# Row maxima transposed before they are split, and eight stores back on one queue, in an attention and Fourier-mixing kernel

## The chip, the cores and the metric

The kernel runs on one core of a Trainium2 chip. The metric is the time of one execution on the device in microseconds (us); of several executions the median counts. Engines are named as the profile names them: PE is TensorE's matmuls, PEld its weight loads, DVE is VectorE, ACT is ScalarE, POOL is GpSimd, SP is SyncE. SPq and ACTq are the queues from which SP and ScalarE issue DMAs. `L735` is line 735 of the kernel before.

## What is computed

Two stages, for a batch of 8, 8 heads, 576 rows, 64 values per head and 128 features. The output has 8 x 576 x 512 fp32 values.

```python
def phi(x):
    proj = np.einsum('bhsd,df->bhsf', x, w_phi)
    proj = proj - np.max(np.abs(proj), axis=-1, keepdims=True)
    return np.concatenate([np.exp(proj), np.exp(-proj)], axis=-1)
q_p, k_p = phi(q), phi(k)
kv  = np.einsum('bhsf,bhsd->bhfd', k_p, v)
num = np.einsum('bhsf,bhfd->bhsd', q_p, kv)
den = np.einsum('bhsf,bhf->bhs', q_p, np.sum(k_p, axis=2))[..., None] + 1e-06
x = (num / den)                      # heads side by side: 8 x 576 x 512
u = x + np.real(np.fft.fft(np.fft.fft(x, axis=1), axis=2))
un = (u - mean(u)) / np.sqrt(var(u) + 1e-06)
out = u + np.maximum(un @ w_ch1, 0.0) @ w_ch2       # 512 -> 2048 -> 512
```

The maximum over the absolute projections of a row is what this change handles: for the queries of the first batch it is needed as a row vector, along the free dimension of a matmul.

## The kernel before

**Stages.** For each of the 8 batches the kernel loads q, k and v, projects them on the features, exponentiates, forms the key-value products per head (tile `kv`, copied to `kvh`), combines them with the queries' features (`pn_`, divided into the tile `X`), folds the rows (`R`, `CEO`), applies the Fourier matrices (`psD`, `pu`), normalises (`UN`, `UT`) and runs the two layers (`psf`, `pso`), whose result is added into `X` and stored.

**Order.** The stages of neighbouring batches are interleaved by a written plan: a string of letters, each of which runs one step of a stream (M mixing, F the two layers, T the features, P the queries' maxima, and so on). A step issues its instructions to the engines in program order; each engine works off its own instructions in that order and waits on semaphores. Y is a step of matmuls whose result nobody reads (tile `idle`).

**Tiles.** PSUM has three pools: `pj` (two buffers), `pk` (one) and `pb` (three). A DMA issued from SP or ScalarE takes one of eight completion semaphores in turn, and waits for the DMA that had it before.

**The first batch** has its own functions, in `first_features`. The queries' negative features are exp(-(proj)) with the maximum taken off twice inside PSUM: `negative` and `last_rows` add, to the projection in `psn` or `ph4`, matmuls that pick a row of maxima (weights `pick`, a column with -2 in three places 32 rows apart, L697 and L717). The maxima come from `widest` and `widest4` (projection `psq`, reduced by L755 and L772 into the fp32 tile `MQ`), for the outer heads (pairs 0 and 3) first and the inner heads (pairs 1 and 2) later. Each time `turn_m` turns the 20 columns of maxima into rows. It splits them into three bf16 parts in SBUF (L730 to L733: high part, remainder, middle part, low part, into the tile `m3`), transposes the three together with one bf16 matmul against the identity (L735, into `pt`), and casts the result into the bf16 tile `mt` (L740). [...] After `turn_m` for the inner heads come, on DVE, the reciprocals and products of the first combines (L951, L953).

**The last batch.** `store` writes rows of `X` when the second layer has been added: chunk 1 in eight DMAs of 64 KB (L1201), chunks 0 and 3 in one of 256 KB with chunk 2 (L1207). In the last batch the eight alternate between SP's and ScalarE's queue:

```python
for a in range(8):
    queue = nc.scalar if b == B - 1 and a % 2 else nc.sync
    queue.dma_start(...)
```

Then follow chunk 3 (L1207 on SP) and the last 64 rows in two halves of 256 columns: `forward` stores the first half from ScalarE and the second from SP (both L1280), with one row of each from ScalarE (L1281).

Of the kernel before, what the change touches and what calls it, by code (L numbers as in the profile page):

```python
# [10 lines left out]
ALU = mybir.AluOpType  # L11
AX = mybir.AxisListType
F32 = mybir.dt.float32
BF16 = mybir.dt.bfloat16
# [26 lines left out]
def kernel(  # L41
# [10 lines left out]
    nc = tc.nc  # L52
    B, H, S, D = q.shape
# [11 lines left out]
    const = ctx.enter_context(tc.tile_pool(name="const", bufs=1))  # L65
# [4 lines left out]
    small = ctx.enter_context(tc.tile_pool(name="small", bufs=2))  # L70
# [4 lines left out]
    pk = ctx.enter_context(tc.tile_pool(name="pk", bufs=1, space=PSUM))  # L75
# [10 lines left out]
    wphi2 = const.tile([128, DF], BF16, name="wphi2")  # L86
# [24 lines left out]
    MQ = [const.tile([128, H, 5], F32, name=f"MQ{i}") for i in range(2)]  # L111
# [13 lines left out]
    ident = const.tile([128, 128], F32, name="ident")  # L125
# [5 lines left out]
    nc.vector.memset(keep[64:65], 0.0)  # L131
    pick_i = const.tile([96, 32], I32, name="pick_i")
    pick = const.tile([96, 32], BF16, name="pick")
    m3 = const.tile([128, 3, 32], BF16, name="m3")
    nc.vector.memset(m3[:], 0.0)
    ident_b = const.tile([128, 128], BF16, name="ident_b")

    def count(out, pattern, base, mult):
# [184 lines left out]
    def load_first():  # L323
# [36 lines left out]
        QT4 = attn.tile([128, 4, 64], BF16, tag="QT4", name="QT4")  # L360
        turned_k[0], turned_q[0] = (KT, KT4), (QT01, QT23, QT4)
        parts[0] = first_features()

    def turn_part(dst, blocks, by_act):
# [271 lines left out]
    def first_features():  # L636
        QT01, QT23, QT4 = turned_q[0]
        KT, KT4 = turned_k[0]
        V, V4_ = values[0]
        mq = MQ[0]  # L640
        KPp = attn.tile([128, H, 4, DF], BF16, tag="KPp", name="KPp")
        KPn = attn.tile([128, H, 4, DF], BF16, tag="KPn", name="KPn")
        K4p = attn.tile([128, 4, DF], BF16, tag="K4p", name="K4p")
# [6 lines left out]
        tiles, rows_of_m = {}, {}  # L650

        def half(x, outer):
            return x[:, 0:4:3] if outer else x[:, 1:3]

        def by_pair(x):
            return x.rearrange("p (x e) n -> p x e n", e=2)

        def project(ps, t, outer, last):
            for x, pr in enumerate((0, 3) if outer else (1, 2)):
                for jj in range(2):  # L660
                    rr = slice(64 * jj, 64 * jj + 64)
                    rq = (QT01, QT23)[t][rr, 2 * pr:2 * pr + 2, :]
                    rq = rq.rearrange("p h (a r) -> p h a r", r=16)
                    rq = rq[:, :, :, ::-1] if t else rq[:, :, ::-1, :]
                    nc.tensor.matmul(
                        ps[:, jj, 2 * x:2 * x + 2, :], lhsT=wphi2[rr, :], rhs=rq,
                        start=last or x == 0, stop=last,
                    )
# [9 lines left out]
        def result(t, outer, QP, ps, sgn):  # L678
            if outer:
                return rows_of(t, outer, QP, ps, sgn)  # L680
            o = QP[:, 2:6, 256 * t:256 * t + 256].rearrange("p h (c s) -> p c h s", c=2)
            nc.scalar.activation(out=o[:, ::-1] if t else o, in_=ps[:], func=AT.Exp, scale=sgn)
# [6 lines left out]
        def negative(t, outer):  # L689
            ps = pj.tile([128, 2, 4, 128], F32, tag="pj", name="psn")  # L690
            project(ps, t, outer, False)
            m = rows_of_m[outer][:].rearrange("p (a r) -> p a r", r=16)
            m = m[:, :, ::-1] if t else m[:, ::-1, :]
            for jj in range(2):
                for x in range(4):
                    k_ = 5 * x + 2 * t + (1 - jj if t else jj)
                    nc.tensor.matmul(  # L697
                        ps[:, jj, x, :], lhsT=pick[:, k_:k_ + 1].to_broadcast([96, 128]), rhs=m,
                        start=False, stop=(x == 3),
                    )  # L700
            result(t, outer, QPHN, ps, -1.0)
# [22 lines left out]
            nc.scalar.activation(out=o, in_=i, func=AT.Exp, scale=sgn)  # L724

        def turn_m(outer):
            m = half(mq[:].rearrange("p (x e) c -> p x (e c)", e=2), outer)
            left = small.tile([128, 2, 10], F32, tag="ml", name="ml")
            hi, mid, lo = (m3[:, i, 0:20].rearrange("p (x n) -> p x n", x=2) for i in range(3))
            nc.vector.tensor_copy(out=hi, in_=m)  # L730
            nc.vector.tensor_tensor(out=left[:], in0=m, in1=hi, op=ALU.subtract)
            nc.vector.tensor_copy(out=mid, in_=left[:])
            nc.vector.tensor_tensor(out=lo, in0=left[:], in1=mid, op=ALU.subtract)  # L733
            pt = pk.tile([96, 128], F32, tag="pk", name="pt")
            nc.tensor.matmul(  # L735
                pt[:], lhsT=m3[:].rearrange("p a b -> p (a b)"), rhs=ident_b[:],
                start=True, stop=True,
            )
            mt_ = small.tile([96, 128], BF16, tag="mt", name="mt")
            nc.vector.tensor_copy(out=mt_[:], in_=pt[:])  # L740
            rows_of_m[outer] = mt_

        def widest(t, outer):
            ps = [pb.tile([128, 4, DF], F32, tag="pb", name="psq") for jj in range(2)]
            for x, pr in enumerate((0, 3) if outer else (1, 2)):
                for e in range(2):
                    for jj in range(2):
                        rr = slice(64 * jj, 64 * jj + 64)
                        nc.tensor.matmul(
                            ps[jj][:, 2 * x + e, :], lhsT=(QT01, QT23)[t][rr, 2 * pr + e, :],  # L750
                            rhs=wphi2[rr, :], start=True, stop=True,
                        )
            for jj in range(2):
                c = 2 * t + (1 - jj if t else jj)
                nc.vector.tensor_reduce(  # L755
                    out=half(by_pair(mq[:])[:, :, :, c], outer),
                    in_=ps[jj][:].rearrange("p (x e) f -> p x e f", e=2), axis=AX.X, op=ALU.max,
                    apply_absolute_value=True,
                )

        def widest4():
            ps = [pb.tile([64, 4, DF], F32, tag="pb", name="psq4") for e in range(2)]
            for pr in range(4):
                for e in range(2):
                    rr = slice(64 * e, 64 * e + 64)
                    nc.tensor.matmul(
                        ps[e][:, pr, :], lhsT=QT4[rr, pr, :], rhs=wphi2[rr, :],
                        start=True, stop=True,
                    )
            m = mq[0:64, :, 4].rearrange("p (pr e) -> p e pr", e=2)  # L770
            for e in range(2):
                nc.vector.tensor_reduce(  # L772
                    out=m[:, e], in_=ps[e][:], axis=AX.X, op=ALU.max, apply_absolute_value=True
                )

        def maxima():
            yield widest(0, True)
            yield widest(1, True)
            yield widest4()
            yield turn_m(True)  # L780
            yield widest(0, False)
            yield widest(1, False)
            yield turn_m(False)
# [32 lines left out]
        def steps():  # L816
            yield keys4()
            for pr in PAIRS:
                yield from keys(pr)
            yield positive(0, True)  # L820
            yield positive(1, True)
            yield last_rows(QPHP, 1.0, None)
            yield negative(0, True)
            yield negative(1, True)
            yield last_rows(QPHN, -1.0, True)
            yield positive(0, False)
            yield positive(1, False)
            yield negative(0, False)
            yield negative(1, False)
            yield last_rows(QPHN, -1.0, False)  # L830
# [366 lines left out]
    def store(b, U, c):  # L1197
        if c == 1:
            for a in range(8):
                queue = nc.scalar if b == B - 1 and a % 2 else nc.sync  # L1200
                queue.dma_start(  # L1201
                    out=out[b, 225 - 32 * a:257 - 32 * a, :].rearrange("(r j) n -> r j n", j=2),
                    in_=U[16 * a:16 * a + 16, 0:2, 0:C],
                )
        elif c in (2, 3):
            rows_ = out[b, 320:576, :].rearrange("(a r j) n -> a r j n", r=16, j=2)
            nc.sync.dma_start(out=rows_[:, ::-1, 3 - c, :], in_=U[:, c, 0:C])  # L1207
        elif c == 4:
            nc.sync.dma_start(out=out[b, 257:320, :], in_=U[1:64, 4, 0:C])
            nc.sync.dma_start(out=out[b, 0:1, :], in_=U[0:1, 4, 0:C])  # L1210

    def forward(b):
# [80 lines left out]
        for g in (0, 64):  # L1293
            nc.vector.scalar_tensor_tensor(
                out=U[0:64, 4, 0:C], in0=po[g:g + 64, :], scalar=scale_of[b, 4][0:64],
                in1=U[0:64, 4, 0:C], op0=ALU.mult, op1=ALU.add,
            )
        store(b, U, 4)
        yield

# [108 lines left out]
```

## Time and profile before

| | |
|---|---|
| median of 3 runs | 426.7 us (426.19 to 426.71) |
| the profiled execution's own time | 426.19 us |
| its span, first to last instruction | 424.3 us |
| PE busy | 399.3 us (94%) |
| PEld busy | 255.9 us (60%) |
| DVE busy | 330.8 us (78%) |
| ACT busy | 306.0 us (72%) |
| POOL busy | 207.8 us (49%) |
| granted TensorE clock, mean | 0.995 |

The span is what the profile covers; the execution's own time is 1.9 us longer. Busy shares are averages over the whole span. The page follows the chain of work that ended last back from the last instruction and gives the shares of its engines. A timeline line has the start and the length in us, the engine, the source line, the operation, the tiles (written <- read), the shapes, and in brackets the idle time of that engine before it with what ended it. For a line that merges several instructions (x8) the length goes from the first start to the last end. The lines of DMA queues give the time that issuing took, not the transfer.

### The profile page before, as it was taken

The numbers are of one execution on the slowest core, as the hardware profiler recorded it, in microseconds if no ns is written. First come the engines' busy times: TensorE is split into PE (matmuls) and PEld (weight loads), VectorE is DVE, ScalarE is ACT, GpSimd is POOL, SyncE is SP. The second block draws the span as 40 slices with busy tenths as digits, with TensorE's granted clock in tenths as the row PEclk, the third lists the DMA queues.
The fourth block names the chain that finished last, engine by engine and source line by source line (L and its number), as shares of the span: only waits on it lengthen the run. The fifth ranks groups of instructions, "written<-read, shape, count | busy, mean of one in ns | idle before, by whom it ended". The sixth has DMA issues, their size and how long they took to land.

```text
span 424.3 us, 10395 instructions
## 1 busy us (share of the span) xinstructions
PE 399.3 (94%) x4093; PEld 255.9 (60%) x4122; DVE 330.8 (78%) x682; ACT 306.0 (72%) x626; POOL 207.8 (49%) x271
## 2 busy tenths in 40 slices
PE   8797798999899999999999999999999999999995
PEld 3365475744676558655676558565766567656562
DVE  4889788798979976998779895998999796968103
ACT  6888799748975899489847887588868887353460
POOL 7983588526656077706682282744755341500000
PEclk9899999999999999999999999999999999999999
DMA  8999949974669459953999059953894051103313
GB/s 218 202 167 174 149 76 170 145 86 78 89 113 179 65 97 109 126 76 56 116 153 126 7 101 127 122 71 62 119 139 76 14 102 32 27 0 72 72 26 87
DMA packets 108699, 42.70 MB, mean 101 GB/s; under 512 B 82859, under 2 KB 103595, under 8 KB 108651
## 3 DMA queue, kind: packets, MB, share of 16 engines
q0 software_dynamic: 45936, 16.60, 35.8%
q1 hardware_dynamic: 62287, 25.05, 33.7%
q8 instruction: 32, 0.52, 0.5%
q10 hardware_dynamic: 428, 0.39, 0.3%
q14 instruction: 16, 0.13, 0.1%
HBM read 36.77 MB, written 9.44 MB: 109 GB/s over the span
## 4 chain that ended last, share of the span: by engine, by line
PE 63%; DVE 22%; ACT 9%; DMA 2%; issue 2%; POOL 0%; DVEq 0%; ACTq 0%
PE psf L1223 21%; PE pso L1240 19%; DVE R L903 3%; DVE cb L999 3%; PE kv L887 3%; PE idle L1340 3%; DVE tg L994 3%; PE psD L1045 2%; DMA UT<-UN 2%; PE pso L1287 2%; PE pu L1104 2%; PE psq L547 1%; DVE MK L511 1%; PE psk L491 1%; PE psh L597 1%
## 5 line engine op out<-in xcount | busy, mean ns | idle before, releaser
L1223 PE MATMUL psf<-UT,W1b 128*128 128x320 bf16 (+1 forms) x1024 | 142.5, 286 | 2.6 <-DMA UT<-UN 1.8
L1240 PE MATMUL pso<-W2b,HT 128*128 128x512 bf16 x483 | 120.6, 379 | 1.7 <-issue 0.5
L1223 PEld LDWEIGHTS <-W1b 128*128 128x128 bf16 x1024 | 94.0, 98 | 29.9 <-issue 4.1
L1240 PEld LDWEIGHTS <-HT 128*128 128x128 bf16 x512 | 46.4, 98 | 46.4 <-issue 2.6
L1228 ACT ACTIVATE HT<-psf 128x320 bf16<-128x320 f32 x128 | 53.5, 442 | 27.0 <-PE psf L1223 21.6
L1002 POOL TENSOR_TENSOR X<-cb,rd 128x320 f32<-128x320 f32 x56 | 41.6, 746 | 39.3 <-DVE rd L1001 38.0
L466 POOL TENSOR_TENSOR VCn<-VS,VCn 128x512 bf16<-128x512 bf16 x28 | 29.7, 1062 | 38.1 <-ACT VCn L461 35.3
L1230 ACT ACTIVATE HT<-psf 128x512 bf16<-128x512 f32 x64 | 37.9, 605 | 12.9 <-PE psf L1223 12.3
L555 DVE TENSOR_REDUCE MQ<-psq 128x8 f32<-128x1024 f32 (+1 forms) x32 | 34.3, 1085 | 13.6 <-PE psq L547 13.4
L1246 DVE SCALAR_TENSOR_TENSOR X<-pso,rs,X 128x512 f32<-128x512 f32 x32 | 23.6, 736 | 24.4 <-PE pso L1240 24.4
L497 ACT ACTIVATE KPn<-psk 128x1024 bf16<-128x1024 f32 x28 | 28.6, 1021 | 14.6 <-DVE MK L511 14.6
L497 ACT ACTIVATE KPp<-psk 128x1024 bf16<-128x1024 f32 x28 | 28.7, 1025 | 11.1 <-PE psk L491 11.1
L451 POOL TENSOR_TENSOR V4N<-VS,V4N 64x256 bf16<-64x256 bf16 x14 | 8.7, 624 | 54.5 <-ACT V4N L447 54.0
L511 DVE TENSOR_REDUCE MK<-psk 128x8 f32<-128x1024 f32 x28 | 33.9, 1213 | 1.0 <-ACT KPp L497 0.7
L1094 DVE TENSOR_TENSOR X<-pu,X 128x512 f32<-128x512 f32 (+3 forms) x49 | 23.3, 526 | 11.2 <-PE pu L1104 8.9
L466 POOL TENSOR_TENSOR VCp<-VS,VCp 128x512 bf16<-128x512 bf16 x28 | 29.7, 1059 | 0.0
L606 ACT ACTIVATE QPHP<-psh 128x1024 bf16<-128x1024 f32 x28 | 28.9, 1031 | 0.8 <-PE psh L597 0.6
L606 ACT ACTIVATE QPHN<-psh 128x1024 bf16<-128x1024 f32 x28 | 29.0, 1035 | 0.0
L1150 ACT ACTIVATE UN<-X,MV 128x512 bf16<-128x512 f32 (+1 forms) x35 | 24.5, 723 | 5.4 <-DVE MV L1175 3.1
L1174 DVE BATCH_NORM_STATS2 st<-X 128x6 f32<-128x512 f32 (+1 forms) x40 | 27.1, 677 | 0.3
L1190 POOL TENSOR_TENSOR rs<-VE,mhalf 128x5 f32<-128x5 f32 (+1 forms) x9 | 10.3, 1142 | 29.2 <-DVE VE L1189 29.0
L987 PEld LDWEIGHTS <-QPHP 128*128 128x128 bf16 x280 | 21.2, 99 | 4.6 <-DVE cb L999 1.0
(465 smaller groups left out, 820.5 us busy)
## 6 DMA issues: line engine op xcount, KB each, us to landing
out_dram<-X SPq DMA_DIRECT2D x16, 256.0 KB
out_dram<-X SPq DMA_DIRECT2D x60, 64.0 KB
QS<-in_q_dram POOLq DMA_DIRECT2D x14, 256.0 KB, 6.0
KS<-in_k_dram POOLq DMA_DIRECT2D x7, 512.0 KB, 6.8
VS<-in_v_dram POOLq DMA_DIRECT2D x14, 256.0 KB, 5.1
W1b<-in_moe_w_ch_dram POOLq DMA_DIRECT2D x1, 2048.0 KB, 13.2
W2b<-in_moe_w_ch_dram POOLq DMA_DIRECT2D x1, 2048.0 KB, 16.4
W2b<-in_k_dram SPq DMA_DIRECT2D x2, 512.0 KB
```

What stands on the lines that cost most here:

```text
L466: nc.gpsimd.tensor_tensor(out=VC[:, hs, :, 0:D], in0=values[b][0][:, hs, :].rearrange("p h (j d) -> p h j d", d=D), in1=VC[:, hs, :, D:D + ...
L497: nc.scalar.activation(out=KP[:, hs, :, :].rearrange("p e (jp jj) f -> p jj (e jp) f", jj=2), in_=psk[:], func=AT.Exp, scale=sgn,)
L511: nc.vector.tensor_reduce(out=MK[:, 2 * pr:2 * pr + 2, :].rearrange("p e (jp jj) -> p jj (e jp)", jj=2), in_=tiles[pr][:], axis=AX.X, op=A ...
L555: nc.vector.tensor_reduce(out=o, in_=i[:], axis=AX.X, op=ALU.max, apply_absolute_value=True)
L606: nc.scalar.activation(out=o, in_=psh[:], func=AT.Exp, scale=sgn)
L1002: nc.gpsimd.tensor_tensor(out=X[:, :, D * h:D * h + D], in0=cb[:, :, 0:D], in1=rd[:].to_broadcast([128, 5, D]), op=ALU.mult,)
L1150: nc.scalar.activation(out=UN[0:M, c, :], in_=X[0:M, c, 0:C], func=AT.Identity, scale=-1.0, bias=mv[0:M, c, 0:1],)
L1174: nc.vector.bn_stats(out=st[0:M, :], in_=X[0:M, c, 0:C])
L1223: nc.tensor.matmul(ps, lhsT=W1b[:, cc, 128 * hh:128 * hh + 128], rhs=UT[:, cc, lo:hi], start=(cc == 0), stop=(cc == NCC - 1),)
L1228: nc.scalar.activation(out=HT[:, hh, lo:hi], in_=ps, func=AT.Relu, scale=-1.0)
L1230: nc.scalar.activation(out=HT[:, hh - 1:hh + 1, lo:hi], in_=psw[:].rearrange("p (a n) -> p a n", a=2), func=AT.Relu, scale=-1.0,)
L1240: nc.tensor.matmul(po[:], lhsT=HT[:, hh, at:at + 128], rhs=W2b[:, hh, :], start=(hh == 0), stop=(hh == NHH - 1),)
```

## The change

Two edits. In the first batch `turn_m` transposes the 20 columns of fp32 maxima first, with a TensorE transpose into PSUM (20 x 128). The split into three bf16 parts is then done on the transposed rows, from PSUM, into rows 0 to 19, 32 to 51 and 64 to 83 of a tile `mt` that is zeroed once at the start; the remainder is written back in place in PSUM. `MQ` of the first batch is viewed with the outer heads' 20 columns together and the inner heads' 20 columns together, and `widest` and `widest4` write it in that order. In the last batch the eight stores of chunk 1 all go to SP's queue.

```diff
-    m3 = const.tile([128, 3, 32], BF16, name="m3")
-    nc.vector.memset(m3[:], 0.0)
+    mt = const.tile([96, 2, 128], BF16, name="mt")
+    nc.vector.memset(mt[:], 0.0)
...
-        mq = MQ[0]
+        mq = MQ[0][:].rearrange("p (o x e) c -> p o x e c", o=2, e=2)
...
-            m = rows_of_m[outer][:].rearrange("p (a r) -> p a r", r=16)
+            m = rows_of_m[outer].rearrange("p (a r) -> p a r", r=16)
...
         def turn_m(outer):
-            m = half(mq[:].rearrange("p (x e) c -> p x (e c)", e=2), outer)
-            left = small.tile([128, 2, 10], F32, tag="ml", name="ml")
-            hi, mid, lo = (m3[:, i, 0:20].rearrange("p (x n) -> p x n", x=2) for i in range(3))
-            nc.vector.tensor_copy(out=hi, in_=m)
-            nc.vector.tensor_tensor(out=left[:], in0=m, in1=hi, op=ALU.subtract)
-            nc.vector.tensor_copy(out=mid, in_=left[:])
-            nc.vector.tensor_tensor(out=lo, in0=left[:], in1=mid, op=ALU.subtract)
-            pt = pk.tile([96, 128], F32, tag="pk", name="pt")
-            nc.tensor.matmul(
-                pt[:], lhsT=m3[:].rearrange("p a b -> p (a b)"), rhs=ident_b[:],
-                start=True, stop=True,
-            )
-            mt_ = small.tile([96, 128], BF16, tag="mt", name="mt")
-            nc.vector.tensor_copy(out=mt_[:], in_=pt[:])
-            rows_of_m[outer] = mt_
+            to = mt[:, 0 if outer else 1, :]
+            pt = pk.tile([20, 128], F32, tag="pk", name="pt")
+            nc.tensor.transpose(
+                pt[:], mq[:, 0 if outer else 1].rearrange("p x e c -> p (x e c)"), ident[:]
+            )
+            nc.vector.tensor_copy(out=to[0:20], in_=pt[:])
+            nc.vector.tensor_tensor(out=pt[:], in0=pt[:], in1=to[0:20], op=ALU.subtract)
+            nc.vector.tensor_copy(out=to[32:52], in_=pt[:])
+            nc.vector.tensor_tensor(out=to[64:84], in0=pt[:], in1=to[32:52], op=ALU.subtract)
+            rows_of_m[outer] = to
...
-                    out=half(by_pair(mq[:])[:, :, :, c], outer),
+                    out=mq[:, 0 if outer else 1, :, :, c],
...
-            for pr in range(4):
+            for x, pr in enumerate((0, 3, 1, 2)):
...
-                        ps[e][:, pr, :], lhsT=QT4[rr, pr, :], rhs=wphi2[rr, :],
+                        ps[e][:, x, :], lhsT=QT4[rr, pr, :], rhs=wphi2[rr, :],
...
-            m = mq[0:64, :, 4].rearrange("p (pr e) -> p e pr", e=2)
+            m = mq[0:64, :, :, :, 4].rearrange("p o x e -> p e (o x)")
...
             for a in range(8):
-                queue = nc.scalar if b == B - 1 and a % 2 else nc.sync
-                queue.dma_start(
+                nc.sync.dma_start(
```

## The prediction

> **What bounds the kernel now.** I read four views: the page's chain that ended last, that chain in order of time for the first 47 us, the timeline of VectorE (DVE) and TensorE (PE) around the two changed steps, and the timeline of the two store queues at the end. The page's chain summary:
>
> ```profile
> PE 63%; DVE 22%; ACT 9%; DMA 2%; issue 2%; POOL 0%; DVEq 0%; ACTq 0%
> ```
>
> TensorE carries the end, so a wait placed in front of TensorE is paid unless something else is later. The chain in order of time (start, us, what) runs through both places where the change works:
>
> ```profile
> 31.64 0.19 PE pt L735
> ...
> 32.47 0.55 PE psn L697 x8
> ...
> 34.53 0.33 PE pn__730 L944 x10
> ...
> 34.88 0.21 DVE rd L951
> ```
>
> Here TensorE works without a hole from 28.06 to 34.86, and then hands the chain to DVE. The timeline (start, us, engine, line; in brackets the idle time before it and who ended it):
>
> ```profile
> 25.41 0.29 DVE L740 CAST mt<-pt 96x128 bf16<-96x128 f32 x1 [0.35 <-PE pt L735]
> ...
> 26.10 0.62 PE L697 MATMUL psn<-mt,pick 96*128 96x128 bf16 x8
> ...
> 28.06 0.29 PE L887 MATMUL kv<-VCp,KPp 128*128 128x65 bf16 x4 [0.21 <-POOL VCp L869]
> ...
> 28.47 0.58 DVE L730 CAST m<-MQ 128x20 bf16<-128x20 f32 x1
> ...
> 29.09 0.98 DVE L731 TENSOR_TENSOR ml<-MQ,m 128x20 f32<-128x20 f32 x1
> ...
> 30.11 0.78 DVE L732 CAST m<-ml 128x20 bf16<-128x20 f32 x1
> ...
> 30.92 0.18 DVE L733 TENSOR_TENSOR m<-ml,m 128x20 bf16<-128x20 f32 x1
> ...
> 31.57 0.26 PE L735 MATMUL pt<-ident_b,m 128*96 128x128 bf16 x1
> ```
>
> The split into three bf16 parts (L730 to L733) is slow the second time, 2.63 us, yet it is over at 31.10 while TensorE comes to its matmul at 31.57; the idle time before L735's weight load is put down to issue, not to DVE. So the split is hidden; only the cast after the matmul (0.29) stands between TensorE's transpose and the matmuls L697 that read the result.
>
> The end:
>
> ```profile
> 414.82 2.56 SPq L1201 DMA_DIRECT2D out_dram<-X  x4
> 414.83 2.86 ACTq L1201 DMA_DIRECT2D out_dram<-X  x4
> 418.28 0.65 SPq L1207 DMA_DIRECT2D out_dram<-X  x1
> 419.53 0.57 ACTq L1280 DMA_DIRECT2D out_dram<-X  x1
> 420.55 0.31 SPq L1280 DMA_DIRECT2D out_dram<-X  x1
> ```
>
> No engine computes after 420.53; the stores' traffic ends at 422.7 in the trace's DMA records and the span at 424.3.
>
> **The change, part by part.** TensorE, GpSimd and ScalarE keep their order in the changed build, apart from the changed instructions; the written plan is the same.
>
> *First batch, outer heads.* The fp32 transpose stands where L735 stood, so TensorE comes to it at 25.11 as before. One fp32 128x128 transpose (L368) is 0.27 us against 0.26 for L735; I take them as equal. DVE, which before did its four small operations from 23.92 to 25.06, now idles until the transpose is done and starts at 25.41. Then come four dependent operations on 20x128 from PSUM in place of one cast. L740 is the nearest row, 0.29; L953, which reads PSUM and SBUF, takes 0.49 for 320 elements, about 1.07 ns more for each element beyond L740's 128, so 0.29 again. Dependent DVE operations follow each other with 0.03 to 0.04 between them (L731, L732, L733 start at 24.45, 24.67, 24.88 and take 0.18). Four: 0.29 + 3 x 0.32 = 1.25, done at 26.66 instead of 25.70. That is 0.96 more behind the transpose. No row shows DVE writing PSUM, or an fp32 subtraction in place there: the low bound is the 20-element row, 3 x 0.22 = 0.65; the high one is the held row L731, 3 x 1.0 = 3.0. I take 0.96, because L740 at 31.87 and L953 at 32.48 ran at 0.29 and 0.49 while GpSimd was issuing DMAs (31.19 to 33.55), the kind of company in which L732 took 0.78.
>
> [...]
>
> L697 needed the result at 26.10 and gets it at 26.70, so TensorE is held 0.6. Queued behind it are the second psq, psn and L697; the second psq also waits for a psq buffer, because the four reductions L755 start at 26.70 instead of 25.95, at most 0.1 more. Then comes L887, which now waits for GpSimd until 28.06 although the weights were ready at 27.63: 0.3 to 0.4 of the delay goes there. I carry 0.3 on.
>
> *First batch, inner heads.* TensorE reaches its transpose at 31.87 (31.57 + 0.3), DVE starts at 32.17 and is done at 33.42; L697 needs it at 32.40 and starts at 33.46: 1.06 late, the 0.3 included. DVE's own queue behind it (L951, L953, L220, to 34.72) has 0.16 idle before L951 at 34.88; it starts at 33.45 instead of 32.18, is free at about 35.8 and the fourth combine comes from TensorE at 35.93. So the chain passes 34.88 about 1.05 late. ScalarE has 1.45 of slack before HI at 41.13, so it does not add; what it waits for there is DVE, late by the same 1.05. All later work hangs on this, so nothing gives it back. The saved weight load and cast shape, the larger memset of mt at 1.04 (TensorE and GpSimd are busy without it) and the new layout of MQ cost nothing; if the memset were on the path it would be about 0.1.
>
> *Last batch.* All eight L1201 go to SP. Each is an issue of 0.6; five of the seven earlier batches show eight in 5.12 to 5.15, with the next L1207 0.1 later. So L1207 is issued at 414.82 + 5.13 + 0.1 = 420.05 instead of 418.28: 1.77 late. Its 256 KB start 1.3 after issue and flow for 2.5 (issued 402.71, traffic 404.04 to 406.54; issued 418.28, 419.56 to 422.12), so to 423.9. The last store (L1280 on SP) shares that queue. It also gets a new wait: in the changed build it takes the semaphore of ScalarE's L1280, and SP waits until that one has landed. ScalarE's was issued at 419.53 and its packets ended at 422.42, partly because L1207's were in front. If it lands at 422.3 to 422.8, SP issues 1.7 to 2.2 later than now, and its data are out 2.2 after that, or a little less with nothing in front. Bounds for this part: 1.2 (only L1207's traffic counts, less what it overlapped with) and 2.3. I take 1.85.
>
> [...]
>
> Sum: 1.05 + 1.85 = 2.9. The profiled execution took 426.19 (span 424.3 and 1.9 around it) and is the fastest of the three; from it 429.1, from the median 426.7 **429.6**, which I give.
>
> **Rivals.**
> 1. *The front is absorbed* (a later stage waits for something that the front does not move, for instance weights): 426.7 + 1.85 = 428.55. Against it: the chain from 34.88 to 110 has only engine work and relative waits. 0.10.
> 2. *The end is hidden*, only the front counts: 427.75. For it: the DMA engines have room at 415 to 416. Against it: the issue rows. 0.08.
> 3. *The clock drops.* The trace grants 0.5 from 17.45 to 20.86, after 3.4 us with only 1.75 of TensorE work; 2.05 did not do it. The hole at 40 to 42 moves by 1 us, and the stretch 41.3 to 44.8 falls from 2.74 to about 1.8. Then what lies on the path behind it (L477 0.42, L1104 0.52) doubles: 430.5. 0.08.
> 4. *Not slower.* The split leaves SBUF, where L731 was held 0.98 instead of 0.18. If DVE and not TensorE's place in the plan sets L735, then the inner step shrinks from 3.69 (28.47 to 32.16) to 0.30 + 1.25, 2.1 less, and the outer from 1.78 by 0.2; with the end's 1.85 that is 426.2, and with the end at its low bound 425.6. The front alone gains if TensorE reaches the inner transpose before 30.6, and makes up for the end if it does so by 29.0; that needs 2.6 us of work ahead of L735 to vanish, and the chain shows that work on TensorE. 0.07.
> 5. *Nothing shows*: both parts hidden, 426.7. 0.03.
>
> **How the numbers follow.** The forecast has 0.64. The range from 427.7 to 430.7 takes in rivals 1 to 3 and the bounds of the end (1.2 to 2.3, so 428.95 to 430.05); the high bound of 3.0 for each step in PSUM, which no row in such company supports, stays outside with rivals 4 and 5. About 0.85 us, 0.2%, can be told from no change. Slower by more: 0.64 + 0.10 + 0.08 + 0.08 = 0.90, less 0.01 for rival 2, which ends near the border, so 0.89; within: that 0.01, rival 5 with 0.03 and 0.03 of rival 4, so 0.07; faster: 0.04, the rest of rival 4.
>
> **What would show it.** Right: DVE idle before the first cast of pt, four rows of about 0.29, L697 at 26.7 and 33.5, L951 for the fourth combine near 35.9, SP with eight issues of 5.1 and its last store after ScalarE's has landed. Wrong: rows of 0.5 or more for the operations in PSUM (then slower still), TensorE at its transposes earlier than 25.1 and 31.5, or traffic that ends as soon after the last sum as now.

## The result

The changed kernel takes 427.75 us (median of 22 runs, 426.92 to 429.44), the kernel before on the same chip 426.24 us (22 runs, 424.91 to 427.29). The ratio is 1.0042, with a 95% interval of 1.0030 to 1.0053: 1.8 us slower, between 1.3 and 2.3 (the means are 1.8 apart, the medians 1.5). The forecast was 2.9 slower, from a base of 426.7. Two executions of one experiment below (e7) ran at granted clocks of 0.555 and 0.654 and are left out of its ratio. In the kernel after, the lines of `turn_m` are L729 and L732 to L735, and later lines have numbers smaller by 5 or 6 (kv L882, reciprocal L946, the stores L1195, L1201, L1274).

The profiled execution after took 427.3 us with a span of 425.5, that is 1.2 more span than before. The page's chain has moved a little from TensorE to DVE, and GpSimd has appeared on it:

```profile
PE 57%; DVE 25%; ACT 7%; POOL 5%; DMA 2%; issue 2%; DVEq 0%; ACTq 0%; POOLq 0%
```

The timeline of the kernel after at the first batch, DVE's and TensorE's lines (start, length, engine, line; in brackets the idle time and who ended it):

```profile
25.36 0.28 DVE L732 CAST mt<-pt 20x128 bf16<-20x128 f32 x1 [3.21 <-PE pt L729]
25.67 0.29 DVE L733 TENSOR_TENSOR pt<-pt,mt 20x128 f32<-20x128 f32 x1
...
26.31 0.28 DVE L735 TENSOR_TENSOR mt<-pt,mt 20x128 bf16<-20x128 f32 x1
26.64 0.61 PE L697 MATMUL psn<-mt,pick 96*128 96x128 bf16 x8 [0.66 <-DVE mt L735]
...
33.37 0.61 PE L697 MATMUL psn<-mt,pick 96*128 96x128 bf16 x8 [0.69 <-DVE mt L735]
...
35.84 0.20 DVE L946 RECIPROCAL rd<-pn__724 128x5 f32<-128x5 f32 x1
```

DVE idles until the transpose is done and then makes four operations of 0.28 to 0.29, as forecast; TensorE is held 0.66 and 0.69, and the chain passes the fourth combine's reciprocal at 35.84 where it passed at 34.88. This 0.96 stays: SP's store at 95.35 stood at 94.39 before, the one at 251.06 at 250.09. But the store at 273.77 stood at 273.81. The front's whole delay is gone by then.

The last batch, SP's and ScalarE's queues after:

```profile
414.77 5.12 SPq L1195 DMA_DIRECT2D out_dram<-X  x8
420.00 0.65 SPq L1201 DMA_DIRECT2D out_dram<-X  x1
421.42 0.30 SPq L1274 DMA_DIRECT2D out_dram<-X  x1
419.48 0.57 ACTq L1274 DMA_DIRECT2D out_dram<-X  x1
420.09 0.65 ACTq L1275 DMA_DIRECT2D out_dram<-X  x2
```

The eight issues take 5.12, the 256 KB store leaves at 420.00 instead of 418.28, SP's last store at 421.42 instead of 420.55. In the trace's landing records the last landing comes at 424.35; before it came at 423.05. So the profiled pair adds up: 0.96 at the front, 1.0 given back between 251 and 274, 1.3 at the end, 1.2 in all.

**Where it is given back.** The timelines of TensorE, GpSimd and DVE between 252 and 268, before:

```profile
252.79 1.48 PE L1223 MATMUL psf<-UT,W1b 128*128 128x256 bf16 x12 [0.80 <-DMA UT<-UN]
263.04 0.72 POOL L284 DMA_DIRECT2D KS<-in_k_dram  x1 [8.01 <-DMA KT<-KS]
...
265.21 1.44 POOL L1002 TENSOR_TENSOR X<-cb,rd 128x320 f32<-128x320 f32 x2
265.27 1.41 DVE L1189 TENSOR_SCALAR VE<-MV 128x5 f32<-128x5 f32 x1
267.83 0.40 PE L491 MATMUL psk<-wphi,KT 64*128 64x128 bf16 x8 [0.66 <-DVE cb L999]
```

And after:

```profile
253.48 1.48 PE L1217 MATMUL psf<-UT,W1b 128*128 128x256 bf16 x12 [0.53 <-DMA UT<-UN]
262.02 0.72 POOL L284 DMA_DIRECT2D KS<-in_k_dram  x1 [6.03 <-DMA KT<-KS]
...
265.96 0.13 DVE L1184 TENSOR_SCALAR VE<-MV 128x5 f32<-128x5 f32 x1
267.79 0.40 PE L491 MATMUL psk<-wphi,KT 64*128 64x128 bf16 x8
```

First, TensorE's wait for the transposed `UT` is 0.80 before and 0.53 after: 0.27. Second, before, GpSimd's prefetch of the next keys waits 8.01 for a transpose (`KT`) to land, until 263.04. The two products into `X` that stand behind it on GpSimd therefore run back to back, from 265.21 to 266.65, just when DVE wants to form `VE`: that operation takes 1.41 in place of the 0.13 it takes after, and TensorE then waits 0.66 for DVE's `cb`. After, the transpose lands 1.02 earlier although everything else is 0.69 later, GpSimd is not behind, and the hold doesn't occur. `VE` ends at 266.68, just after the second product. What held it is not in the trace.

The question for the experiments is whether the change did this or chance, and what the two halves cost in the median.

### The profile page after: what moved, and what is told of

Its sections match the earlier page's. It is cut to its first block, busy times and chain, and to the rows that moved or that the text cites. A ratio compares the mean times of both kernels' runs of the same rounds, so it can differ in the third digit from the quotient of the medians.

```text
span 425.5 us, 10392 instructions
## 1 busy us (share of the span) xinstructions
PE 396.9 (93%) x4093; PEld 255.3 (60%) x4122; DVE 327.6 (77%) x680; ACT 306.2 (72%) x626; POOL 207.6 (49%) x271
## 4 chain that ended last, share of the span: by engine, by line
PE 57%; DVE 25%; ACT 7%; POOL 5%; DMA 2%; issue 2%; DVEq 0%; ACTq 0%; POOLq 0%
PE psf L1217 19%; PE pso L1234 18%; DVE R L898 4%; DVE cb L994 3%; PE kv L882 3%; DVE tg L989 3%; DVE MK L511 2%; DMA UT<-UN 2%; PE pso L1281 2%; PE psD L1040 2%; PE pu L1099 2%; DVE CEO L1029 1%; PE psq L547 1%; DVE MQ L555 1%; PE psh L597 1%
```

## The experiments

Times are medians; ratios are to runs of the kernel before taken along with each kernel on the same chip, with 95% intervals; e1 to e4 shared one chip, e5 to e8 another, e9 to e12 a third. The ratios are not those of the two medians, and the two can differ by some tenths of a microsecond. I also compare executions by the start times of ScalarE's 623 instructions, which stand in the same order in all kernels: the difference is a curve of how late one execution runs against another, and its steps show where something is lost or given back.

**The halves alone.** `e1_front` has only the first edit, `e2_end` only the second:

```diff
 # e1_front
-            pt = pk.tile([96, 128], F32, tag="pk", name="pt")
...
+            nc.tensor.transpose(
+                pt[:], mq[:, 0 if outer else 1].rearrange("p x e c -> p (x e c)"), ident[:]
+            )
 # e2_end
-                queue = nc.scalar if b == B - 1 and a % 2 else nc.sync
-                queue.dma_start(
+                nc.sync.dma_start(
```

Expected of e1_front: 

> Only the first-batch edit (fp32 transpose, split in PSUM); the eight stores alternate between two queues as before. Theory A (lost and regained by accident): the 0.96 us of the front is regained behind 250 us, 0.27 at the TensorE wait for UT and 0.69 because VectorE's VE, held 1.41 us beside GpSimd in before, takes 0.13: span and time within 0.3 us of before, VE row near 266 at 0.13 to 0.2. Theory B (carried, as forecast; the pair of profiled executions is an accident): +0.9 to +1.1 us. Theory C (something that the front does not move, a load or a fixed stage, sets the order after 266): 0, with TensorE rows after 270 at the same times as before whatever VE takes.

Expected of e2_end: 

> Only the last-batch edit: all eight stores of chunk 1 on SP, front as before. Theory A: the end costs what the changed kernel's profile shows, 1.2 to 1.4 us, set by the 256 KB of the next store issued 1.7 later. Forecast: 1.85 (1.2 to 2.3). If issuing on one queue is hidden: 0 to 0.2. Its front is that of before, so its VE row near 265 tells whether the hold of 1.41 us comes again: A and B with a hold in every execution, an accident if it is 0.13 to 0.2.

Measured: e1_front 426.84, ratio 1.0019 (1.0005 to 1.0033), 0.8 us; e2_end 426.99, ratio 1.0024 (1.0009 to 1.0040), 1.0 us; before 426.25. The sum, 1.8, is that of the change. Neither half is free, so "the front is absorbed" (theory C) falls for the median, and so does "issuing on one queue is hidden". The decisive row is DVE's in the timeline of e2_end, which has the front of before:

```profile
265.76 0.13 DVE L1189 TENSOR_SCALAR VE<-MV 128x5 f32<-128x5 f32 x1
```

There is no hold here, without the front edit. The 0.69 was a misfortune of the one execution of before that was profiled; in the later executions `VE` took 0.13 to 0.17. By the curve e1_front is 0.96 late behind 33 us and 0.86 at 254 and, because before loses its 0.69 there, 0.18 at 272.

The profiled execution of before has a second accident: its clock was granted at half from 17.45 to 20.86, which cost it 0.2, and neither e2_end's nor that of the changed kernel has such a stretch. So the pair to compare is e2_end and after, which differ by the front alone: there the delay is 1.14 behind 33 us, and of it 0.93 is left at 180, 0.78 at 207 and 0.20 behind 260, although neither has the hold at `VE`. The last step, 0.57, is TensorE's wait for `UT`, 1.10 in e2_end and 0.53 in after:

```profile
253.28 1.49 PE L1222 MATMUL psf<-UT,W1b 128*128 128x256 bf16 x12 [1.10 <-DMA UT<-UN]
```

**Take the hold away.** `e3_ve_early` forms `VE` four microseconds earlier, behind the last measure of each batch; `e4_front_ve` adds the first edit:

```diff
                 measure(b, c)
+                if c == 4:
+                    VE = small.tile([128, 5], F32, tag="VE5", name="VE5")
+                    nc.vector.tensor_single_scalar(out=VE[:], in_=mv[:, :, 1], scalar=1e-06, op=ALU.add)
+                    early[b] = VE
```

Expected of e3_ve_early: 

> Kernel before, but VectorE forms VE (variance plus epsilon) right behind the last measure of a batch, some 4 us earlier, when GpSimd is idle. Theory A: the hold of 1.28 us at 265 goes and TensorE's key projections there start 0.69 earlier: -0.5 to -0.7 us. Theory C: 0, since a stage that VE does not move sets what follows. Theory B says nothing of this kernel beyond 0 if the hold is no part of the path.

Expected of e4_front_ve: 

> The first-batch edit together with the earlier VE, stores as before. Theory A: with no hold to lose the front's delay has little to regain, so against e3 it costs 0.7 to 1.0 us, and against the kernel before +0.0 to +0.4. Theory B: +1.0 against e3. Theory C: 0 against both.

Measured: e3 425.75, ratio 0.9992 (0.9976 to 1.0009), which doesn't show a gain; e4 426.75, 1.0014 (0.9998 to 1.0030). Between the two lies 1.0, the front, without an interval of its own. And the profiled execution of e3 shows the same kind of accident at another place (timeline, GpSimd and DVE):

```profile
227.95 0.89 POOL L284 DMA_DIRECT2D QS<-in_q_dram  x1 [2.79 <-DMA QT<-QS]
228.85 0.74 POOL L1002 TENSOR_TENSOR X<-cb,rd 128x320 f32<-128x320 f32 x1
229.62 1.29 DVE L903 TENSOR_TENSOR R<-X 128x512 f32<-128x512 f32 x2 [1.24 <-POOL X L1002]
```

A prefetch on GpSimd waits 2.79 for a transpose to land, the product behind it comes late, DVE waits 1.24 for it, and the whole kernel is 1.2 later from there on. In before the same prefetch did not wait. So a likely common cause is one step earlier than `VE`: GpSimd's products stand behind issues that wait for landings, and those differ from execution to execution (the keys' prefetch left at 260.69, 261.81, 262.02, 262.20, 262.54 and 263.04 in six of them).

**Take the cause away.** `e5_late_loads` moves two prefetches in the written plan, K behind the scales (from 788 to behind 812 in the string) and Q behind one product (681 to behind 692); `e6_front_late` adds the first edit:

```diff
-    "...FFTFFFQMFFFFTDDFRFFFFTFDP"
+    "...FFTFFFMFFFFTDDFRFQFFFTFDP"
...
-    "...FFMFFTPFMKFFFMFFQPNMF"
-    "FMAUKFFMFFFMTTFRFRFM..."
+    "...FFMFFTPFMFFFMFFQPNMFF"
+    "MAUKFFMFFFMTKTFRFRFM..."
```

Expected of e5_late_loads: 

> Kernel before with two of GpSimd's prefetches issued later: the K loads near 263 behind the scales and two X products, the Q load near 225 behind one X product, so that GpSimd's products no longer stand behind an issue that waits for a transpose to land. Theory A (what differs between executions comes from these waits: 1.24 us lost at 230 in one execution, 0.69 at 268 in another): median 0.3 to 0.9 us below before, less spread, TensorE after 271 at 0.7 to 0.9 earlier than in the profiled execution of before. Theory C (a fixed stage sets what follows): 0. Rival: the moved loads land too late for the next batch and cost more than they give.

Expected of e6_front_late: 

> The first-batch edit with the same later prefetches as the kernel that moves only these, stores as before. Theory A (the front's delay is kept unless a wait for a landing absorbs or hides it): 0.9 to 1.1 above the kernel with the later prefetches alone. Theory C (absorbed by a stage that it does not move): 0 against it.

Measured: e5 425.47, ratio 0.9982 (0.9969 to 0.9996), and ten of its eleven executions lie between 425.04 and 425.56, where those of before spread from 424.98 to 428.12. This is a version that beats both kernels. e6 takes 426.63, 1.0015 (0.9999 to 1.0030): its median is 1.16 higher on this quieter base. That median lies in a gap. Six executions of e6 take 425.78 to 426.23 at granted clocks of 0.996 to 1.000, the other six 427.04 to 427.95 at 0.993 to 0.996; so one half lies 0.3 to 0.8 above e5's median and the other 1.6 to 2.5. The lower clocks point at half-clock stretches in the slower half (below), but none of these was traced. In the two profiled executions, whose times are 0.28 apart, the front's delay is 1.14 at 33 us, 0.82 at 161, 0.52 at 207 and 0.37 from 254 on. It shrinks where TensorE waits in front of the matmuls that read `UT`: 0.27, 1.08 and 0.69 at 158, 206 and 253 in e5, against 0.78 and 0.55 at the last two in e6; a late kernel waits less. At 253 that wait is 0.69 to 1.10 in the seven profiled executions without the front edit, and 0.53 to 0.75 in the five with the edit as it stands.

**The end.** Four kernels take the end apart, on the front of before. `e7_chunk3_gpsimd` issues the 256 KB store from GpSimd; `e8_row0_once` stores row 0 in one piece, which shifts the completion semaphores so that SP's last store no longer waits for ScalarE's half (0.7 in after and in e2_end):

```diff
 # e7_chunk3_gpsimd
-            nc.sync.dma_start(out=rows_[:, ::-1, 3 - c, :], in_=U[:, c, 0:C])
+            queue = nc.gpsimd if b == B - 1 and c == 3 else nc.sync
+            queue.dma_start(out=rows_[:, ::-1, 3 - c, :], in_=U[:, c, 0:C])
 # e8_row0_once
-                nc.scalar.dma_start(out=out[b, 0:1, at:at + 256], in_=U[0:1, 4, at:at + 256])
+                if at:
+                    nc.scalar.dma_start(out=out[b, 0:1, :], in_=U[0:1, 4, 0:C])
```

Expected of e7_chunk3_gpsimd: 

> The last-batch edit alone (eight stores on SP), with the 256 KB store of chunk 3 taken from behind them on SP and issued by GpSimd, which is idle then. Theory A (its place behind eight issues is the price): the 1.35 to 1.5 us of the end seen in the traces fall to 0 to 0.4; the last landing comes 4.5 to 4.9 us after VectorE's last group of sums begins, where it was 4.5 to 4.55 with two queues and 5.9 to 6.0 with one. Rival (the eight stores' own traffic, later by 2 us on one queue, or the wait for ScalarE's half, sets the end): still 5.6 or more.

Expected of e8_row0_once: 

> The last-batch edit alone, with row 0 stored once as 2 KB in place of twice 1 KB, which gives the last store of SP another semaphore and so takes away its wait for ScalarE's half. Theory A (the 256 KB store ahead of it on the queue sets the end): SP issues its last store at once after the last sum, 0.7 earlier, and the end gains 0 to 0.4 of its 1.4. Rival, as in the forecast (the new wait sets the end): 0.7 or more gained.

e7 has a ratio of 1.0052 (1.0034 to 1.0071), from four executions. Theory A's gain would have brought it near 1.000, so the time speaks against that gain; whether a store issued from GpSimd has a price of its own is open, since the profiled execution had a granted clock of 0.555 (span 655.1) and its rows can't be set beside the others. e8 took 427.86, 1.0041 (1.0017 to 1.0064): no gain. Its timeline, SP's queue:

```profile
420.04 0.65 SPq L1206 DMA_DIRECT2D out_dram<-X  x1
420.79 0.42 SPq L1279 DMA_DIRECT2D out_dram<-X  x1
```

The last store leaves 0.10 behind the 256 KB store, without the wait. Yet the last landing comes 6.04 after DVE begins its last group of sums; with the wait it is 5.90 to 6.02 (after, e2, e9, e11). So the new wait, which the forecast made part of the price, costs nothing: the last store lands 0.3 behind the 256 KB store with the wait (424.35 and 424.07 in after) and without it (424.52 and 424.23 in e8). With two queues the same interval is 4.49 to 4.60 in seven executions. (e8's median is 0.9 above e2's, on another chip; its end doesn't explain that.)

The other two stand on the quieter base. `e9_end_late` is e5 with eight stores on SP; `e10_six_then_chunk3` puts the 256 KB store behind the sixth of the eight, with row 0 in one piece:

```diff
+        if c == 1:
+            eight(range(8 if b < B - 1 else 6))
         elif c in (2, 3):
...
+            if b == B - 1 and c == 3:
+                eight((6, 7))
```

Expected of e9_end_late: 

> The kernel with the later prefetches (425.47 us, ten of its eleven executions within 0.5) and the last-batch edit on top: a quieter base on which to weigh the end. From the traces, in which the last landing comes 4.5 to 4.6 us after VectorE's last sums begin with two queues and 5.9 to 6.0 with one: +1.4, 426.9. Rival (part of it is hidden in most executions, as the medians of the single edits on the old base suggest): +0.7 to +0.9. Forecast: +1.85.

Expected of e10_six_then_chunk3: 

> As the kernel with the later prefetches and all eight stores on SP, but the 256 KB store of chunk 3 is issued after six of the eight, and row 0 is stored once as 2 KB so that SP's last store doesn't wait for ScalarE's half. Nothing changes in the number of bytes or in the one queue. Theory A (the place of the 256 KB behind eight issues is the price): chunk 3 issued at about 418 on the base's clock, 1.3 earlier, and the end gains 0.9 to 1.3 of its 1.4. Rival (one queue for all 64 KB stores is the price): 0 to 0.3 gained.

Measured: e9 426.56, ratio 1.0015 (0.9996 to 1.0035), 1.09 above e5's median (1.4 by the ratios, since the two ran on different chips); e10 426.21, 1.0014 (0.9996 to 1.0033), 0.35 less than e9 in the median but the same in the ratio, so that the times show no gain. SP's queue in the timeline of e10:

```profile
413.89 3.84 SPq L1200 DMA_DIRECT2D out_dram<-X  x6
417.84 0.65 SPq L1208 DMA_DIRECT2D out_dram<-X  x1
418.53 2.06 SPq L1200 DMA_DIRECT2D out_dram<-X  x2
420.69 0.44 SPq L1283 DMA_DIRECT2D out_dram<-X  x1
```

The 256 KB store now leaves 0.5 after its sum (DVE's ends at 417.32), and the last landing comes 5.66 after DVE's last sums begin: 0.3 of the 1.4 is regained, not 0.9 to 1.3. For now SP's last store stands behind two more issues and leaves 1.1 after the last sum (DVE's ends at 419.59). Of the two, the first took 0.57, about as the six before, and the second 1.44; such long issues stand elsewhere too (below), and what held this one is open. So e10 doesn't settle how much of the price is the place of the 256 KB: with a second issue of 0.6 the last store would have left some 0.8 earlier, an estimate. What it does show is that the queue has ten issues to make in either order, 6.1 us (e2_end) to 7.0 (here) of issuing, while the last sum is done 5.7 after the first of them. That this is the rest of the price is argued, not shown.

**Both on the quieter base, and a larger dose.** `e11_both_late` is the changed kernel with the later prefetches; `e12_front_dose` is e6 with the first PSUM copy made five times:

```diff
 # e12_front_dose
-            nc.vector.tensor_copy(out=to[0:20], in_=pt[:])
+            for again in range(5):
+                nc.vector.tensor_copy(out=to[0:20], in_=pt[:])
```

Expected of e11_both_late: 

> The changed kernel itself with the later prefetches. Theory A (front and end add, each carried): against the later prefetches alone +0.7 to +1.1 for the front and +1.4 for the end, 427.5 to 428.0. Rival, front absorbed: 426.9, as with the end alone.

Expected of e12_front_dose: 

> The first-batch edit with the later prefetches, and in each of its two steps the first PSUM copy is made five times in place of once: four more VectorE operations of 0.31, 1.25 us a step. Theory A (a delay of the front is carried but for what a later wait for a landing takes up, 0.3 to 0.6): +2.2 to +2.5 against the same kernel with single copies, TensorE 3.3 to 3.5 late at 33 us and 2.6 or more late at the end. Theory C (absorbed): under +0.5. Rival (a TensorE hole of nearly 3 us drops the clock): a half-clock stretch of 3.4 us near 35 to 45 and more than +3.

Measured: e11 427.96, ratio 1.0043 (1.0026 to 1.0061). Against e9 that is 1.40 for the front, against e6 1.33 for the end, against e5 2.5 for both (1.2, 1.2 and 2.6 by the ratios; e5 and e6 ran on another chip). But the profiled executions of e11 and e9 take 428.00 and 427.99: both had a half-clock stretch near 42 to 48, e9's cost 1.5, and behind it the front's delay is 0.6 and at the end 0.06. Most other executions of e9 are over a microsecond faster than its profiled one, those of e11 are not; so the 1.40 may in part be clock. e12 took 431.46, 1.0123 (1.0096 to 1.0150): 4.8 more than e6 for a dose of 2.5 (4.6 by the ratios). By the curve it is 2.50 later than e6 before the window below, 3.0 behind it and 3.9 at the end; a part of the rest is what e6 gives back on the way and e12 keeps. The table of windows shows the step from 2.5 to 3.0 (us, PE busy, PEld, DVE, ACT, POOL, granted TensorE clock, DMA share, GB/s):

```profile
34.16:37.57 3.41, 1.71 (x36) 1.44 (x36) 2.67 (x11) 1.35 (x2) 0.00 (x0) 1.00 1.79 174
37.57:40.98 3.41, 3.41 (x53) 3.00 (x51) 3.11 (x8) 2.52 (x3) 0.00 (x0) 0.50 1.49 126
```

Behind the larger hole the clock stood at half for 3.41 us, as the third rival has it; the dose itself was carried, not absorbed. The difference of the medians is 0.9 above that of the profiled executions; that part is open.

## Why the prediction was right or wrong

- **The front's operations and its two steps: right.** 0.28 to 0.29 for each operation (0.29 forecast), L697 at 26.64 and 33.37 (26.70 and 33.46), the reciprocal at 35.84 (35.93). The times agree this well in part by luck, since the forecast started from an execution that had lost 0.2 to its clock; beside e2_end the delay is 1.14.
- **Its size: right behind the two steps; at the end only the medians agree.** 1.05 was forecast, and four profiled pairs (e3 and e4, e2 and after, e5 and e6, e9 and e11) show 1.07 to 1.16 behind 33 us. In time the four pairs of kernels give 0.8 (0.2 to 1.4, e1 by its ratio) and, in the medians, 1.0, 1.16 and 1.40. But e2 and after, and e5 and e6, keep only 0.20 and 0.37 of it to the end in their profiled executions. So the medians hold something that these don't show; half-clock stretches are a candidate, and that is not shown.
- **"All later work hangs on this, so nothing gives it back": wrong as a statement.** Between 158 and 254 us one pair of executions (e5, e6) gives back 0.77 of 1.14, nearly all of it where TensorE waits in front of the matmuls that read `UT`, after gives back 0.94 of its 1.14 against e2_end, and the profiled pair before and after gives back all 0.96, of which 0.69 was an accident of before's. I had read the chain only from 34.88 to 110. Rival 1, which I gave 0.10, describes these pairs but not the medians.
- **The end: right in place, its term too large.** The 256 KB store left at 420.00 (420.05 forecast) and its traffic ended at 423.7 (423.9). The term that failed is the new wait: I let ScalarE's half land at 422.3 to 422.8; it landed at 421.4, with the 256 KB issued behind it (420.00 against 419.48) and no longer ahead of it (418.28 against 419.53 before). SP issued 0.87 later instead of 1.7 to 2.2, and e8 shows that even this cost nothing. The traces give 1.3 to 1.5 where I had 1.85; the times 1.0 (e2, by its ratio) and, in the medians, 1.09 (e9 against e5) and 1.33 (e11 against e6). That the end costs nothing is excluded by e2's interval, 1.0009 to 1.0040.
- **The rivals.** The end is not hidden (2). The clock (3) did not drop in the changed kernel's profiled execution while TensorE worked, but it did in e9_end_late, without the first edit, and in e11_both_late, with both (0.50 for 3.41 us, below). DVE's place (4) was as the forecast had it: TensorE's plan sets the transposes.
- **The sum.** With the end at 1.4 the same sum is 2.45, and on the quieter base both together measure 2.5. On the kernel as it is they measure 1.8 (1.3 to 2.3). The measured 427.75 lies only 0.05 inside the range, which began at 427.7, and it equals rival 2's figure by accident: both parts cost something. The base was too high as well, 426.7 from three executions where 22 gave 426.24. Where the missing 0.7 goes in the median, in the waits that differ from execution to execution or in the spread of the measurement, is open.

## What to carry to other kernels

A delay on the chain was carried here through engine work, but waits for a DMA's landing took some of it up (at `UT`, 1.10 in e2_end and 0.53 in after), so read the chain to its end before writing that nothing gives it back. One profiled execution holds accidents: a row ten times as long as its eight sisters (1.41 beside 0.13 to 0.17) is to be asked about before a difference is built on it. A median can lie between two groups of executions, as e6's does, so look at the single times too. And compute that stood behind a prefetch on GpSimd's queue inherited that prefetch's wait (1.24 in e3): moving two prefetches behind the products gave 0.8 us (0.2 to 1.3).

## What the runs showed of the hardware

- **The half-clock stretches of these runs lie on a grid of 3.41 us.** The seven seen in the first 50 us (one each in before, e3, e4, e9 and e11, two in e12) are 3.41 us long and begin at whole multiples of 3.41 from the start of the clock record (in before the record starts at 7.21, the stretch at 17.45; the two of e12, at 17.09 and 37.57, are six times 3.41 apart). TensorE's hole that ends at 41.68 in e9_end_late and at 42.83 in e6_front_late is 1.80 long in both; where it falls in the grid differs. e9_end_late, with the front of before, and e1_front, with the edit, in the table of windows:

```profile
38.66:42.08 3.42, 1.56 (x7) 0.58 (x6) 3.38 (x10) 1.98 (x5) 0.20 (x1) 1.00 0.94 195
42.08:45.49 3.41, 3.35 (x8) 0.88 (x7) 3.31 (x9) 0.18 (x1) 3.22 (x7) 0.50 0.95 134
```

```profile
39.40:42.82 3.42, 1.59 (x7) 0.55 (x6) 3.39 (x9) 1.98 (x5) 0.73 (x1) 1.00 1.03 203
42.82:46.23 3.41, 3.27 (x23) 1.62 (x22) 3.31 (x9) 1.12 (x2) 3.22 (x9) 1.00 1.00 134
```

  With 1.56 us of work in the window, 46% of it, the next one has half the clock, and e9 is 1.5 late behind it; with 1.59, 1.61 and 1.62 (e1, e2, e6) nothing happens. e11 fell too (1.56). So an execution with or without the edit can lose this. Busy time alone is not the measure, though: near 15 us windows with 1.68 to 1.92 of work were followed by half the clock (e3, before, e12, e4), and near 25 us windows with 1.79 and 1.82 (e6, e12) were not. What else counts is open.
- **Now and then a single issue is long.** In seven profiled executions (before, after, e2, e8 to e11) a 64 KB store from SP took 0.57 to 0.70 to issue, but one near 151 us and one near 388 took 1.2 to 1.7 in each, and the second behind the 256 KB store in e10 took 1.44. Why is open.
- **One DVE operation on 128x5 took ten times as long beside two GpSimd products**: 1.41 for 0.13, in the one profiled execution of before.
